# Two last products of a range's blocks done together in seven half products, in a fused attention and feed-forward kernel

## The chip, the cores and the metric

The kernel runs on one core of a Trainium2 chip. The metric is the device time of one execution in microseconds, the median of several runs; lower is better. A profile of one execution is read beside it: what each engine did and when. The engines are PE (TensorE, the matrix multiplier; its weight loads are listed as PEld), DVE (VectorE), ACT (ScalarE), POOL (GpSimd) and SP (SyncE, which here only issues DMA transfers). Each engine works through its own queue of instructions in order and waits for others by semaphores.

## What is computed

Attention over 8 batches of 12 heads, 448 positions and 64 channels, followed by a feed-forward layer with a leaky ReLU:

```python
def _attn_ref(q, k, v):
    scores = (1.0 / np.sqrt(q.shape[-1])) * np.matmul(q, k.transpose(0, 1, 3, 2))
    scores = scores - np.max(scores, axis=-1, keepdims=True)
    attn = np.exp(scores)
    attn = attn / (np.sum(attn, axis=-1, keepdims=True) + 1e-09)
    return np.matmul(attn, v).astype(np.float32)

def _moe_ref(x, w_in, w_out):
    h = x @ w_in                       # 3584 x 768 by 768 x 2048
    g = np.maximum(0.01 * h, h)
    return (g @ w_out).astype(np.float32)   # 3584 x 2048 by 2048 x 768

# x is the attention's output, (batch, position) by (head, channel)
```

Inputs and output are float32; the kernel multiplies in bfloat16 and sums in float32.

## The kernel before

**Ranges.** The 3584 tokens are cut into seven ranges (`cuts`, line 41: 0, 640, 1152, 1664, 2176, 2688, 3072, 3584). A range goes through the first layer (`head` and `neck` for range 0, `hidden(i)` for the others) and then through the second (`second(i)`). The attention of later batches is laid between the matmuls of the second layer: bursts of scores (`scores`, line 306), their exponentials on ACT (`expo`), and rows (`rows`, line 857: the weighted sums on PE, then a reciprocal and a product on DVE, then a DMA transpose from SP's queue into `xT`). `place` (line 968) decides where, with a small clock of its own, `model`, that counts what PE is given. A burst is laid only where all three slots are there and free. The kernel is written for one fixed order: each engine gets its instructions as the Python code emits them.

**PSUM.** Two single banks `g0` and `g1` (`banks`, line 66) and three tiles of two banks each, `sc0` to `sc2` (`slots`, line 67). Scores and rows use the slots, the second layer the banks, the first layer both.

**The second layer.** Blocks of 128 tokens are taken two at a time (`spots`, line 487: two pairs in each of ranges 1 to 6). For a pair, the product of 256 x 2048 by 2048 x 768 is cut in two along tokens, inner dimension and columns, and done by seven products in place of eight (the scheme of Strassen and Winograd), in `block_pair` (line 592). Each product is 8 matmuls of 128 x 128 by 128 x 384, in two accumulators `b` and `a` that alternate between the two banks. Sums of weights (`w_mix`, made once by `mix_weights` on DVE) and sums of `h` (`h_mix`, `mix_h`, and lines 621 and 627) stand in for the plain blocks. After each product DVE copies the bank to the output tile (`keep`, line 613) or adds it there (`join`, line 616), and finished tiles are stored (`store`, line 388). The seventh product multiplies the lower half of h of the pair's second block by `t4`, the third sum of weights (line 658), into the left half of the second block's output. In the last pair of all it is done in two halves of 192 columns, so that the last store is small (lines 649 to 656). Range 0 has one such pair and one done plainly (`plain_pair`).

**The first layer.** `hidden` (line 512) does the same with w_in: groups of products of 6 matmuls in two chains, one over the two banks and one over two slots, with rows laid between. Its sums of x (`x_mix`, `mix_x_part`, line 466: differences on DVE, some of 512 columns, some of 256) are emitted inside the second layer of the range before, where `model` says that the transposes of x have landed, in two parts; what is left is emitted at its end.

**The ring of x.** `xT` holds the transposed attention output, 768 channels by tokens, as a ring of `NX` = 15 x 128 tokens for each of 6 groups of 128 channels (line 103). A batch's sequence of 448 tokens that crosses the ring's end runs over into the next group's row and is copied back to the front (`OVER`, lines 108 and 469 to 473; 128 columns, emitted by `mix_x_part(3)` in the second layer of range 2).

Of the kernel before, what the change touches and what calls it, by code (L numbers as in the profile page):

```python
# [9 lines left out]
F32 = mybir.dt.float32  # L10
BF16 = mybir.dt.bfloat16
# [5 lines left out]
def kernel(  # L17
# [9 lines left out]
    nc = tc.nc  # L27

    B, H, S, D = q.shape
    DM, DF = moe_w_in.shape  # L30
    P = 128
# [4 lines left out]
    MD = DF // P  # L36
    NW = DM // 2
# [4 lines left out]
    NR = len(cuts) - 1  # L42
# [57 lines left out]
    qkb = [qkb_all[:, i] for i in range(NB)]  # L100


    NX = 15 * P

    def place_of(t):
        return (t + NX - cuts[3]) % NX

    OVER = -cuts[3] % S
    xT_flat = xT_pool.tile([P, KD * NX + OVER], BF16, name="xT")
    xT = xT_flat[:, :KD * NX].rearrange("p (k t) -> p k t", k=KD)  # L110

# [1 line left out]
    w_out_sb = w_pool.tile([P, MD, DM], BF16)  # L113
    MH = MD // 2
    w_mix = w_pool.tile([P, 3, MH, NW], BF16)
    KEEP = 4
    h = h_pool.tile([P, MD, (KEEP + 1) * P], BF16, name="h")
    h_mix = h_pool.tile([P, MH, 2, P], BF16, name="hmix")
# [305 lines left out]
    def mix_weights():  # L424
# [14 lines left out]
        for lo, hi in pieces:  # L439
            nc.vector.tensor_sub(w_out_sb[:, lo, right], w_out_sb[:, lo, right], w_out_sb[:, lo, left])  # L440
            yield

    def mix_w_in():

        near, far = slice(0, KH), slice(KH, KD)
        pieces = [(ts(c, 2 * P), slice(FH + 2 * c * P, FH + 2 * (c + 1) * P)) for c in range(FH // (2 * P))]
        for lo, hi in pieces:
            s2, s3, s4 = (w_in_mix[:, x, :, lo] for x in range(3))
            for o, x, y in (
                (s3, w_in_sb[:, near, lo], w_in_sb[:, near, hi]),  # L450
                (s2, w_in_sb[:, far, hi], s3),
                (s4, w_in_sb[:, far, lo], s2),
            ):
                nc.vector.tensor_sub(o, x, y)
                yield
        yield
        for lo, hi in pieces:
            nc.vector.tensor_add(w_in_sb[:, near, hi], w_in_sb[:, near, hi], w_in_sb[:, far, hi])
            yield
# [6 lines left out]
    def mix_x_part(i, ks):  # L466

        at = place_of(cuts[i])
        if at == 0:
            for hp in range(KD - 1) if ks.start == 0 else (KD - 1,):  # L470
                nc.vector.tensor_copy(xT[:, hp, :OVER], xT_flat[:, (hp + 1) * NX:(hp + 1) * NX + OVER])
                if hp in (1, KD - 2, KD - 1):
                    yield
        nh = (cuts[i + 1] - cuts[i]) // 2
        near, far = slice(ks.start, ks.stop), slice(KH + ks.start, KH + ks.stop)
        one, two = slice(at, at + nh), slice(at + nh, at + 2 * nh)
        t2, t3, t4 = (x_mix[:, x, near, :nh] for x in range(3))
        for o, x, y in (
            (t3, xT[:, far, two], xT[:, near, two]),
            (xT[:, near, two], xT[:, near, two], xT[:, near, one]),  # L480
            (t2, xT[:, far, two], xT[:, near, two]),
            (t4, xT[:, far, one], t2),
        ):
            nc.vector.tensor_sub(o, x, y)
            yield

    def spots(i):

        if i == 0:
            return 0, [(0, 1), (2, 3)]  # L490
        return 0, [(0, 2), (1, 3)] if cuts[i + 1] - cuts[i] == 4 * P else [(0, 1), (KEEP, 2)]

    def token(i, x):

        return KEEP * P if x == KEEP else cuts[i] + x * P

# [15 lines left out]
    def hidden(i):  # L512
# [76 lines left out]
        for m in ready:  # L589
            mix_h(i, m)  # L590

    def block_pair(i, c):

        lo, hi = slice(0, MH), slice(MH, MD)
        x1, x2 = spots(i)[1][c]
        one, two = ts(x1, P), ts(x2, P)
        s3 = h_mix[:, :, c]
        t2, t3, t4 = (w_mix[:, x] for x in range(3))
        t1 = w_out_sb[:, lo, NW:]
        left, right = slice(0, NW), slice(NW, DM)  # L600
        o1 = o_pool.tile([P, DM], F32, name="o")
        o2 = o_pool.tile([P, DM], F32, name="o")
        b, a = banks

        def product(ps, x, w, first=False, cols=slice(0, NW)):
            for m in range(MH):
                if m in (2, 4, 6):
                    yield
                nc.tensor.matmul(  # L609
                    ps[:, cols], x[:, m], w[:, m], start=(first and m == 0), stop=(m == MH - 1), skip_group_check=True,  # L610
                )

        def keep(o, at, ps, by=nc.vector.tensor_copy):
            by(o[:, at], ps[:, :NW])  # L614

        def join(o, at, ps):
            nc.vector.tensor_add(o[:, at], o[:, at], ps[:, :NW])  # L617

        yield
        yield from product(b, h[:, lo, one], w_out_sb[:, lo, left], first=True)  # L620
        nc.vector.tensor_sub(h[:, lo, one], h[:, lo, two], h[:, lo, one])
        short = cuts[i + 1] - cuts[i] < 4 * P
        keep(o1, left, b, nc.scalar.copy if c == 0 and (short or i + 1 == NR) else nc.vector.tensor_copy)
        yield
        yield from product(a, h[:, hi, one], w_out_sb[:, hi, left], first=True)
        join(o1, left, a)
        nc.vector.tensor_sub(h[:, hi, one], h[:, hi, one], h[:, lo, one])
        yield
        yield from product(b, h[:, lo, one], t2)
        keep(o1, right, b)  # L630
        yield
        yield from product(a, h[:, lo, two], t1, first=True)
        keep(o2, right, a)
        yield
        yield from product(b, s3, t3)
        join(o2, right, b)
        yield
        t0 = token(i, x2)
        last = t0 + P == B * S
        if last:  # L640
            nc.vector.tensor_copy(o2[:, NW // 2:NW], b[:, NW // 2:NW])
            store(o1, token(i, x1), left)
            store(o2, t0, right)
        yield from product(a, h[:, hi, one], w_out_sb[:, hi, right])
        join(o1, right, a)
        store(o1, token(i, x1), right if last else slice(0, DM), (nc.sync, nc.scalar if last else nc.sync))
        yield
        if last:
            w1, w2 = slice(0, NW // 2), slice(NW // 2, NW)
            yield from product(b, h[:, hi, two], t4[:, :, w1], cols=w1)  # L650
            nc.vector.tensor_copy(o2[:, w1], b[:, w1])
            store(o2, t0, w1, (nc.scalar, nc.sync))
            end = slots[0][:, 0]
            yield from product(end, h[:, hi, two], t4[:, :, w2], first=True, cols=w2)
            nc.vector.tensor_add(o2[:, w2], o2[:, w2], end[:, w2])
            store(o2, t0, w2, (nc.sync, nc.scalar))
            return
        yield from product(b, h[:, hi, two], t4)
        keep(o2, left, b)
        store(o2, t0)  # L660
        banks.reverse()
# [369 lines left out]
    def second(i):  # L1031

        x_sums = [mix_x_part(i + 1, slice(0, 2)), mix_x_part(i + 1, slice(2, 3))] if i + 1 < NR else []
        fresh, summed = [None, None], [i + 1 == NR] * 2
        left = plan[i]
        for c in range(len(spots(i)[1])):
            whole = c < plain(i)
            for x, _ in enumerate((plain_pair if whole else block_pair)(i, c)):
                fine = 1 if whole else 2
                if x % (2 * fine) == 0:  # L1040
                    advance(all(summed) or rows_done < need[i + 2])
                if c or x:
                    model["now"] += 0.65 / fine
                left -= place(i, left, calm=whole or x not in ((1, 2, 3) if i == 5 else (1, 2)), keen=need[min(i + 2, NR)], cap=NU if all(summed) else need[i + 2])
                turn_next(i)
                if whole and x in (1, 3, 5, 7):
                    mix_h(i, x - 1)
                if whole and x in (8, 9, 11, 13, 15):
                    next(outs)
                if i == 0 and c and x % 4 == 2:  # L1050
                    next(ins, None)
                for y in range(2):
                    if fresh[y] is None and i + 1 < NR and rows_done >= need[i + 2] - 1 + y:
                        fresh[y] = model["now"] + 7.0
                for y, todo in enumerate(x_sums if x % fine == 0 else ()):
                    if fresh[y] is not None and fresh[y] <= model["now"] and not summed[y]:
                        summed[y] = next(todo, 0) is not None
                        if not summed[y]:
                            break
        assert left == 0 or nxt == NU, (i, left)  # L1060
        assert i + 1 == NR or rows_done >= need[i + 2], (i, rows_done)
        for todo in x_sums:
            for _ in todo:
                pass

    ins, outs = mix_w_in(), mix_weights()
    early = [1, 2, 4, 6, 7, 9, 11]
    goals = [1, 4]
    groups, done = 0, 0
# [60 lines left out]
```

## Time and profile before

| | |
|---|---|
| time, median of 3 runs | 382.67 us (382.62 to 383.18) |
| span of the profiled execution, first to last instruction | 381.0 us |
| TensorE clock granted | 1.00 throughout |
| second layer's matmuls in pairs of blocks (L609) | 720 of 384 columns and 16 of 192; 32% of the chain |
| DVE busy | 229.9 us, of it 18 us the sums of x (L484) |
| POOL | casts of q, k, v and their loads until about 305 us of the span, then nothing |
| from the last matmul of 192 columns to the end of the span | 3.6 us: a sum on DVE (0.35), a store's issue (0.3), its landing (1.8 from its issue), the closing of the program (1.3) |

How to read the lines that follow: in the page's list of groups, a line is "line of the code, engine, operation, output<-input, shapes, count | busy us in total, mean ns of one | idle time of the engine just before them <- who ended it". In a timeline it is "start us, length us, engine, line, operation, count [idle before <- who ended it]". Matmuls are pipelined: the rows of a queue of matmuls overlap, and the pace is read from the starts. Names of buffers are shown without their numbers: `g` is a bank, `sc` a slot, `o` an output tile.

### The profile page before, as it was taken

What the parts mean: (1) busy time and instruction counts of PE and PEld (TensorE: products, weight loads), DVE (VectorE), ACT (ScalarE), POOL (GpSimd) and SP (SyncE); (2) the same over time, 40 slices, a digit from 0 to 9 for tenths busy, and PEclk for the clock granted to TensorE, in tenths of its full rate; (3) what the DMA queues carried; (4) which work ended last, traced back from release to release, by engine and by line L of the source; (5) the groups of instructions that cost most, each with busy time, mean ns of one, the idle gap of its engine ahead of it and who ended that gap; (6) DMA issues with size and microseconds to landing.
All of it is one profiled execution on the core that took longest, in us unless ns stands there. A gap on an engine that the chain in (4) does not pass through costs nothing.

```text
span 381.0 us, 9888 instructions
## 1 busy us (share of the span) xinstructions
PE 373.0 (98%) x3944; PEld 262.3 (69%) x3944; DVE 229.9 (60%) x488; ACT 254.9 (67%) x391; POOL 183.7 (48%) x376
## 2 busy tenths in 40 slices
PE   7899999999999999999999999999999999999996
PEld 3665657766598656886658866588665895668854
DVE  5663847445766646566476573765736665474753
ACT  5998885765848876478764878638787388617700
POOL 8988820996979456760576603848027100000000
PEclk9999999999999999999999999999999999999999
DMA  9999999699999759991499915999139800330022
GB/s 159 200 201 203 180 191 181 90 170 203 144 168 157 101 102 161 206 129 28 87 172 197 145 28 67 174 202 146 25 68 192 147 14 2 80 109 29 2 82 85
DMA packets 99294, 47.84 MB, mean 126 GB/s; under 512 B 63664, under 2 KB 95920, under 8 KB 99248
## 3 DMA queue, kind: packets, MB, share of 16 engines
q0 software_dynamic: 40384, 22.47, 47.9%
q1 hardware_dynamic: 58608, 24.52, 33.0%
q8 instruction: 31, 0.51, 0.5%
q10 hardware_dynamic: 256, 0.22, 0.2%
q14 instruction: 15, 0.12, 0.1%
HBM read 45.61 MB, written 11.01 MB: 149 GB/s over the span
## 4 chain that ended last, share of the span: by engine, by line
PE 93%; ACT 4%; DMA 1%; issue 1%; DVE 0%; ACTq 0%; DVEq 0%
PE g L609 32%; PE g L537 14%; PE sc L537 14%; PE sc L317 7%; PE sc L345 6%; PE g L419 4%; PE sc L314 4%; PE sc L357 3%; PE g L674 3%; ACT e L326 3%; PE g L715 2%; PE sc L338 2%; PE g L296 1%; DMA w_in_mix<-in_k_dram 1%; PE g L357 1%; ACT c L329 1%
## 5 line engine op out<-in xcount | busy, mean ns | idle before, releaser
L326 ACT ACTIVATE e<-sc 128x896 bf16<-128x896 f32 (+1 forms) x144 | 123.9, 930 | 34.0 <-PE sc L317 20.4
L609 PEld LDWEIGHTS <-h 128*128 128x128 bf16 x632 | 59.3, 98 | 44.7 <-issue 9.3
L609 PE MATMUL g<-w_out_sb,h 128*128 128x384 bf16 x416 | 78.7, 326 | 0.0
L184 POOL COPY qkb<-fq 112x512 bf16<-112x512 bf16 x36 | 24.0, 665 | 90.7 <-DMA qkT<-qkb 74.9
L526 ACT ACTIVATE h<-c 128x512 bf16<-128x512 f32 (+1 forms) x72 | 43.5, 611 | 25.2 <-DVE c L552 15.8
L537 PEld LDWEIGHTS <-w_in_sb 128*128 128x128 bf16 x576 | 54.3, 98 | 5.9
L537 PEld LDWEIGHTS <-w_in_mix 128*128 128x128 bf16 x432 | 41.2, 98 | 4.1
L873 DVE RECIPROCAL rec<-sc 112x8 f32<-112x8 f32 x42 | 8.7, 207 | 54.2 <-PE sc L345 25.9
L609 PE MATMUL g<-w_mix,h 128*128 128x384 bf16 (+1 forms) x208 | 39.0, 323 | 0.0
L614 DVE COPY o<-g 128x384 f32<-128x384 f32 x49 | 27.1, 552 | 10.4 <-PE g L609 10.1
L345 PE MATMUL sc<-v,e 128*128 128x65 bf16 x720 | 33.3, 193 | 0.0
L317 PE MATMUL sc<-qkT 64*128 64x448 bf16 (+1 forms) x210 | 32.8, 352 | 0.0
L345 PEld LDWEIGHTS <-e 128*128 128x128 bf16 x720 | 31.1, 98 | 1.4
L617 DVE TENSOR_TENSOR o<-o,g 128x384 f32<-128x384 f32 x39 | 21.6, 554 | 16.3 <-PE g L609 15.3
L874 DVE TENSOR_TENSOR x<-sc,rec 112x512 bf16<-112x512 f32 x42 | 29.0, 691 | 1.5
L537 PE MATMUL sc<-xT,w_in_sb 128*128 128x256 bf16 (+1 forms) x216 | 28.5, 268 | 0.0
L537 PE MATMUL g<-xT,w_in_sb 128*128 128x256 bf16 (+1 forms) x216 | 28.5, 268 | 0.0
L549 ACT COPY c<-g 128x512 f32<-128x512 f32 (+1 forms) x12 | 6.8, 569 | 30.8 <-PE g L537 30.8
L338 PE MATMUL sc<-v,e 128*128 128x130 bf16 x120 | 26.5, 220 | 0.0
L157 POOL DMA_DIRECT2D fv<-in_v_dram x33 | 20.6, 631 | 4.1 <-POOL v L197 2.4
L314 PE MATMUL sc<-qkT 64*128 64x448 bf16 x144 | 19.9, 357 | 2.1 <-ACT e L326 1.0
L357 PEld LDWEIGHTS <-e 112*128 112x128 bf16 x432 | 20.0, 98 | 1.8 <-issue 0.4
(131 smaller groups left out, 684.0 us busy)
## 6 DMA issues: line engine op xcount, KB each, us to landing
fq<-in_q_dram POOLq DMA_DIRECT2D x18, 224.0 KB, 5.9
w_in_sb<-in_moe_w_in_dram POOLq DMA_DIRECT2D x4, 768.0 KB, 11.2
w_out_sb<-in_moe_w_out_dram POOLq DMA_DIRECT2D x4, 768.0 KB, 19.5
out_dram<-o SPq DMA_DIRECT2D x7, 336.0 KB, 3.4
out_dram<-o SPq DMA_DIRECT2D x8, 288.0 KB, 4.0
fk<-in_k_dram POOLq DMA_DIRECT2D x15, 128.0 KB, 5.7
fv<-in_v_dram POOLq DMA_DIRECT2D x15, 128.0 KB, 4.1
out_dram<-o SPq DMA_DIRECT2D x7, 240.0 KB, 3.4
```

Of the source, the lines that this page charges most:

```text
L184: by(t[:SC, x].rearrange("p so h d -> p h so d"), f)
L314: nc.tensor.matmul(ps[:, j, :S], t[p, S + c * SC:S + c * SC + P], t[p, :S], start=True, stop=True)
L317: nc.tensor.matmul(ps[:, j, :S].rearrange("p (so s) -> p so s", so=NSC), t[p, 1, c], t[p, 0, :, :SC], start=True, stop=True,)
L326: nc.scalar.activation(e[:, :, c, :], ps[:n, :, :S], AX.Exp, scale=scale)
L338: nc.tensor.matmul(ps, e[:, EM + qc * SC:EM + qc * SC + P], vt[:, 2 * KC:].rearrange("p j d -> p (j d)"), start=True, stop=False, skip_gro ...
L345: nc.tensor.matmul(ps[:, j * (D + 1):(j + 1) * (D + 1)], e[:, at:at + P], vt[:, j * KC + c], start=False, stop=(c == KC - 1), skip_group_c ...
L357: nc.tensor.matmul(ps[:, qc, :], t[:SC, at:at + P], vt[:, c], start=(c == 0), stop=(c == NSC - 1),)
L526: nc.scalar.activation(hs[:, m:m + 2, cols], x.rearrange("p (m t) -> p m t", m=2), AX.Prelu, alpha=0.01)
L537: nc.tensor.matmul(ps[:, j * nh:(j + 1) * nh], w[:, kk, ts(j, P)], x[:, kk], start=(first and j == 0 and kk == 0), stop=(kk == KH - 1), sk ...
L609: nc.tensor.matmul(ps[:, cols], x[:, m], w[:, m], start=(first and m == 0), stop=(m == MH - 1), skip_group_check=True,)
L614: by(o[:, at], ps[:, :NW])
L874: nc.vector.tensor_mul(x, ps[:, :, :, :D], rec.to_broadcast([SC, 2, 2 * NP, D]))
```

## The change

In ranges 1 to 6 the seventh products of the two pairs share their weights, `t4`: together they are one product of 256 tokens by 1024 by 384. The change does it by seven half products once more (`deep`): each is 4 matmuls of 128 x 128 by 128 x 192, 28 in all, in place of 16 of 384 columns. The two accumulators of `deep` are the two banks of one slot, which is taken out of `slots` for that time, so that no scores are laid there. They are laid between the matmuls of the fifth and sixth product of the second pair, one half product after every two matmuls of 384 columns (in range 6 the sixth product is done in two halves of 192 columns, with its own order). After each half product DVE adds 128 x 192 numbers to an output tile.

The weights' sums for it (`mix_deep`) are made once, on POOL, in the second layer of range 1: four operations of 768 columns. The sums of h (`deep_sums`) are three DVE operations of 512 columns per range, emitted in the sixth product of the first pair, and a fourth comes in `deep`. After its fifth product a pair copies the accumulator `b` to the left half of its second output tile, where the seventh product was copied before. The first pair's second tile is kept (`kept`) until `deep` has added its part, and is stored then; its left half in range 6 goes out by POOL's queue. The order of the stores in range 6 is new.

The ring of x has 12 blocks instead of 15, and its places are counted from `cuts[5]`. The sequence that crosses the ring's end is now the third (tokens 896 to 1343, at 1152): 192 columns are copied back, in `mix_x_part(2)`, emitted in the second layer of range 1. At token 2688 the ring begins anew at the start of a sequence, without copies.

```diff
-    NX = 15 * P
+    NX = 12 * P
     def place_of(t):
-        return (t + NX - cuts[3]) % NX
+        return (t - cuts[5]) % NX
...
+    QH, QW = MH // 2, NW // 2
+    deep_mix = w_pool.tile([P, 3, QH, QW], BF16)
...
+    def mix_deep():
+        t, (t2, t3, t4) = w_mix[:, 2], (deep_mix[:, x] for x in range(3))
+        lo, hi, left, right = slice(0, QH), slice(QH, MH), slice(0, QW), slice(QW, NW)
+        sub, add = nc.gpsimd.tensor_sub, nc.gpsimd.tensor_add
+        for by, o, x, y in (
+            (sub, t3, t[:, hi, right], t[:, lo, right]),
+            (add, t2, t3, t[:, lo, left]),
+            (sub, t4, t[:, hi, left], t2),
+            (sub, t[:, lo, right], t[:, lo, right], t[:, lo, left]),
+        ):
+            by(o, x, y)
+            yield
...
+    def deep_sums(i):
+        one, two = (ts(x[1], P) for x in spots(i)[1])
+        lo, hi = slice(MH, MH + QH), slice(MH + QH, MD)
+        s3, s1 = h_mix[:, :QH, 0], h_mix[:, QH:, 0]
+        for by, o, x, y in (
+            (nc.vector.tensor_sub, s3, h[:, lo, one], h[:, lo, two]),
+            (nc.vector.tensor_add, h[:, lo, two], h[:, lo, two], h[:, hi, two]),
+            (nc.vector.tensor_sub, s1, h[:, lo, two], h[:, lo, one]),
+        ):
+            by(o, x, y)
+            yield
+
+    def deep(i):
...
+        o = [kept[i, c] for c in range(2)]
+        end = i + 1 == NR
+        slot = slots.pop(0)
+        b, a = (slot[:, x, :QW] for x in range(2))
+        for ps, first, x, w, c, cols in (
+            (b, True, h[:, lo, one], t[:, :QH, left], 0, left),
+            (a, True, h[:, hi, one], t[:, QH:, left], 0, left),
+            (b, False, s1, t2, 0, right),
+            (a, True, h[:, lo, two], t[:, :QH, right], 1, right),
+            (b, False, s3, t3, 1, right),
+            (a, False, h[:, hi, one], t[:, QH:, right], 0, right),
+            (b, False, h[:, hi, two], t4, 1, left),
+        ):
+            for m in range(QH):
+                nc.tensor.matmul(ps, x[:, m], w[:, m], start=(first and m == 0), stop=(m == QH - 1), skip_group_check=True)
+            nc.vector.tensor_add(o[c][:, cols], o[c][:, cols], ps)
+            if ps is a and first and c == 0:
+                nc.vector.tensor_sub(h[:, hi, one], h[:, hi, one], s1)
+            t0 = token(i, spots(i)[1][c][1])
+            if ps is a and not first:
+                store(o[0], t0, slice(0, NW) if end else slice(0, DM), (nc.gpsimd, nc.gpsimd) if end else (nc.sync, nc.sync))
+            if end and c == 1 and ps is b:
+                store(o[1], t0, cols, (nc.sync, nc.scalar))
+            yield
+        if not end:
+            store(o[1], token(i, spots(i)[1][1][1]))
+        slots.append(slot)
...
-        yield from product(b, s3, t3)
-        join(o2, right, b)
+        def fifth():
+            yield from product(b, s3, t3)
+            join(o2, right, b)
+            if i:
+                keep(o2, left, b)
+                if last:
+                    store(o1, token(i, x1), left)
+                    store(o2, t0, right, (nc.sync, nc.scalar))
+                elif i + 1 == NR:
+                    store(o2, t0, right)
+
+        def sixth():
+            if not last:
+                yield from product(a, h[:, hi, one], w_out_sb[:, hi, right])
+                join(o1, right, a)
+                store(o1, token(i, x1))
+                return
+            for x in range(2):
+                cols = ts(x, QW)
+                for m in range(MH):
+                    if m == QH or x and m == 0:
+                        yield
+                    nc.tensor.matmul(
+                        a[:, cols], h[:, hi, one][:, m], w_out_sb[:, hi, right][:, m, cols], start=False, stop=(m == MH - 1),
+                        skip_group_check=True,
+                    )
+                at = slice(NW + x * QW, NW + (x + 1) * QW)
+                nc.vector.tensor_add(o1[:, at], o1[:, at], a[:, cols])
+                store(o1, token(i, x1), at, (nc.sync, nc.scalar))
+
+        if i and c:
+            more = deep(i)
+            for x, _ in enumerate(fifth()):
+                yield
+                next(more)
+                yield
+            yield
+            for x, _ in enumerate(sixth()):
+                yield
+                if not last or x != 1:
+                    next(more)
+                    yield
+            yield
+            for _ in more:
+                yield
+            return
+        yield from fifth()
+        yield
+        sums = deep_sums(i) if i else ()
+        for _ in sixth():
+            next(sums, None) if i else None
+            yield
+        if i:
+            return
```

More of the change, by code (lines that the diff above doesn't have):

```diff
@@ L100 @@
     qkb = [qkb_all[:, i] for i in range(NB)]
-    NX = 15 * P
+    NX = 12 * P
     def place_of(t):
-        return (t + NX - cuts[3]) % NX
-    OVER = -cuts[3] % S
+        return (t - cuts[5]) % NX
+    OVER = max(-t % S for t in cuts if place_of(t) == 0)
     xT_flat = xT_pool.tile([P, KD * NX + OVER], BF16, name="xT")
@@ L468, in mix_x_part @@
         at = place_of(cuts[i])
-        if at == 0:
+        if at == 0 and cuts[i] % S:
             for hp in range(KD - 1) if ks.start == 0 else (KD - 1,):
@@ L590, in hidden @@
             mix_h(i, m)
+    kept = {}
+    def deep_sums(i):
[10 more added lines that the diff above has]
+    def deep(i):
+        one, two = (ts(x[1], P) for x in spots(i)[1])
+        lo, hi = slice(MH, MH + QH), slice(MH + QH, MD)
+        s3, s1 = h_mix[:, :QH, 0], h_mix[:, QH:, 0]
+        t, (t2, t3, t4) = w_mix[:, 2], (deep_mix[:, x] for x in range(3))
+        left, right = slice(0, QW), slice(QW, NW)
+        o = [kept[i, c] for c in range(2)]
[25 more added lines that the diff above has]
+        slots.append(slot)
+        model["free"][id(slot)] = model["now"] + 1.2
     def block_pair(i, c):
@@ L601, in block_pair @@
         o1 = o_pool.tile([P, DM], F32, name="o")
-        o2 = o_pool.tile([P, DM], F32, name="o")
+        o2 = kept[i, c] = o_pool.tile([P, DM], F32, name="o")
         b, a = banks
+        t0 = token(i, x2)
+        last = t0 + P == B * S
         def product(ps, x, w, first=False, cols=slice(0, NW)):
@@ L634, in block_pair @@
         yield
-        yield from product(b, s3, t3)
-        join(o2, right, b)
-        yield
[L638 to L646, printed above, removed]
@@ L647, in block_pair @@
-        yield
[L648 to L657, printed above, removed]
+        def fifth():
[8 more added lines that the diff above has]
+                    store(o2, t0, right)
@@ L1051, in second @@
                     next(ins, None)
+                if i == 1 and not c and x % 4 == 2:
+                    next(deeps, None)
                 for y in range(2):
@@ L1064, in second @@
                 pass
-    ins, outs = mix_w_in(), mix_weights()
+    ins, outs, deeps = mix_w_in(), mix_weights(), mix_deep()
     early = [1, 2, 4, 6, 7, 9, 11]
```

## The prediction

> **What bounds the kernel now.** I read the page's busy times and its shares of the chain first, then the chain in order of time, the timelines of single stretches, and the groups by shape.
>
> ```profile
> PE 373.0 (98%) x3944; PEld 262.3 (69%) x3944; DVE 229.9 (60%) x488; ACT 254.9 (67%) x391; POOL 183.7 (48%) x376
> ...
> PE 93%; ACT 4%; DMA 1%; issue 1%; DVE 0%; ACTq 0%; DVEq 0%
> ```
>
> TensorE (PE) is busy for 98% of the span and is 93% of the chain; VectorE (DVE) is 60% busy and 0% of it. So a matmul that goes saves its own time, and any wait that PE gets is lost in full. The chain in order of time (start, length, what) gives the pace of the matmuls:
>
> ```profile
> 62.90 1.82 PE g L715 x22
> ...
> 244.86 5.53 PE g L609 x34
> ...
> 376.72 0.67 PE sc L609 x8
> 377.40 0.02 issue
> 377.42 0.35 DVE o L655
> ```
>
> A matmul of 384 columns costs 5.53/34 = 0.1625 us, one of 192 columns 1.82/22 or 0.67/8 = 0.083 us. The second row is one whole end of a range (about 244.9 to 250.4), in which PE never waits. Next, how quickly work passes between PE and DVE (start, length, engine, line):
>
> ```profile
> 13.16 0.42 DVE L370 TENSOR_TENSOR x<-g,rec 112x256 bf16<-112x256 f32 x1
> 13.64 0.37 PE L384 MATMUL g<-ident,x 112*128 112x112 bf16 x4 [0.25 <-DVE x L370]
> ```
> ```profile
> 376.56 0.82 PE L609 MATMUL sc<-w_mix,h 128*128 128x192 bf16 x8
> 377.42 0.35 DVE L655 TENSOR_TENSOR o<-o,sc 128x192 f32<-128x192 f32 x1 [0.30 <-PE sc L609]
> ```
>
> PE starts 0.05 us after the DVE result that it waits for (13.58 to 13.64). DVE starts 0.04 us after the end of the last matmul's row (377.38), and that row, a pipeline's depth included, reaches 0.16 us beyond the 0.083 that PE is held. So a sum starts 0.20 us after PE has gone on. DVE in the end of a range:
>
> ```profile
> 245.23 0.56 DVE L614 COPY o<-g 128x384 f32<-128x384 f32 x1 [1.11 <-PE g L609]
> 245.70 0.41 DVE L484 TENSOR_TENSOR x_mix<-xT 128x512 bf16<-128x512 bf16 x1
> 246.15 0.61 DVE L484 TENSOR_TENSOR xT<-xT 128x512 bf16<-128x512 bf16 x1
> ...
> 251.16 0.29 DVE L484 TENSOR_TENSOR x_mix<-xT 128x256 bf16<-128x256 bf16 x1 [1.48 <-DMA xT<-x]
> ```
>
> DVE spends this end on the next range's x sums too. A row that needs nothing of the one before starts 0.08 us before that one's end (245.79 to 245.70), one that does starts 0.03 after it. The last row shows x sums waiting for a transpose, with the later rows of DVE's queue behind them. The shapes that the change uses:
>
> ```profile
> L509 DVE TENSOR_TENSOR hmix<-h 128x512 bf16<-128x512 bf16 x24 | 10.8, 452 | 1.3 <-ACT h L526 0.9
> L471 DVE COPY xT<-xT 128x128 bf16<-128x128 bf16 x6 | 1.3, 214 | 0.1
> L655 DVE TENSOR_TENSOR o<-o,sc 128x192 f32<-128x192 f32 x1 | 0.4, 354 | 0.3 <-PE sc L609 0.3
> ```
>
> **The change part by part.** I call the pairs' products P1 to P7 and the seven half products D1 to D7. In each of ranges 1 to 6 two P7 go, 16 matmuls of 0.1625 = 2.60 us. D1 to D7 come, 28 of 0.0825 = 2.31 us (0.0865, the slowest long run of the first layer's 192 wide matmuls, makes 2.42). The gain is 0.29 us a range, 1.7 in all.
>
> **The new wait.** D1 to D7 alternate between two accumulators, but both are halves of one tile, `slot`. In the program as built the first matmul of each half product waits for the DVE sum that read the half product before it (D2 for D1's, though D2 writes the other half; only D1 has no such wait). Everything behind it in PE's queue waits too. From the end of a D on PE to the earliest next D it is 0.20 + 0.355 (row L655) + 0.05 = 0.605 us; between them lie two matmuls of 384, 0.325. That alone leaves 0.28 us of idle PE five times a range (the gap D3 to D4 has four matmuls).
>
> DVE's queue makes it longer. I count from P5's start in the second pair. In ranges 2 to 4 DVE does, in this order: the copy after P4 (0.20 to 0.76), x sum (to 1.10), sum 1 (1.02 to 1.37), x sum (to 1.75), sum 2, the correction of h (0.45), x sum, sum 3, x sum, P5's join and copy (0.555 each), sum 4, sum 5, x sum, sum 6, P6's join, sum 7. So D2 starts at 1.42, not 0.98; sum 2 is 1.95 to 2.31 and D3 starts at 2.35; sum 3 ends at 3.29, in time for D4 at 3.34; sum 4 stands behind an x sum, join and copy (3.21 to 4.58) and ends at 4.96, so D5 starts at 5.01; sum 5 ends at 5.90, D6 5.95; sum 6 at 6.84, D7 6.89 to 7.22. Without waits D7 would end at 4.91. Stall 2.31, less 0.29: **+2.02 us** each, 6.1 for three. The x sum before sum 6 needs the transpose that landed 4.8 us after P5's start in the row above; one product less stands between, so 6.1 here, and D6's end rules sum 6 all the same.
>
> Range 1 has in addition the copies at the ring's seam, moved there: five of 0.25 us (192 columns, from the 0.214 of 128) before sum 3, one more later. The same count gives a stall of 2.75, **+2.46**. The old seam copies in range 2 were hidden, so taking them away gives nothing. In range 5 the x sums stand later: stall 2.04, **+1.75**. Range 6 has none, but P6 is split and its second half waits for the sum of its first, which stands behind join, copy and sum 4 (4.79, not 3.28): D7 ends at 7.32, sum 7 at 7.88. Before, the same stretch took 1.30 + 1.30 + 0.66 + 0.66 + 0.55 = 4.47, and the first pair's P7 1.30: 5.77. So **+2.10**.
>
> Between the pairs of range 6, where no attention work lies, DVE has join and copy of P5 and three sums of h (0.45 each) before P6's join. That ends 3.03 us after P5; P2 of the second pair needs that bank at 2.60. **+0.48**. In ranges 1 to 5 rows and scores (3.3 us or more) cover it; without that cover it would be 0.5 each.
>
> **The last store.** The first pair's last left half is now stored from Pool's queue, two issues. These are the only rows of such issues, the casting loads:
>
> ```profile
> L157 POOL DMA_DIRECT2D fv<-in_v_dram x33: 610/617/721, 31.7 to 289.0; - x33
> ...
> DMA to landing us min/median/max: 2.9/5.9/22.1
> ```
>
> The second issue starts at 6.94 + 0.66 = 7.6. With the least landing, 2.9, it is down at 10.5; the last SP store (sum 7 at 7.88, then 0.03, and 1.83 to landing as in the last row before) at 9.74. **+0.8**; bounds 0 (lands like SP's) and 3.8 (the median 5.9). I take the quiet end, since the queue is empty by then. The Trainium skill, "DMA: Bandwidth & Descriptors", section "Anatomy of one DMA — SWDGE (gpsimd) path", gives 2.0 us plus bytes over 436 GB/s, for 147 KB an estimate of 2.3 us. By it this term would be 0.2 and the time 0.6 lower; no run here shows a store from that queue.
>
> **At nothing.** In ranges 1 to 5 the first pair's second store moves from its P7 to D6 in SP's queue: two issues of some 0.5 us, right ahead of the second pair's own; behind them stand transposes of rows that the next range's first layer doesn't read. The output tile is held longer, but its buffer is next written in the next range's second layer, over 15 us on. ACT gets one store more at the end (0.38 us, idle there). Four weight sums go to Pool in range 1, where it idles 9.5 of 23.1 us; no row has their form. By the copies of 112x512 (0.61) they cost 4 to 8 us of Pool, ahead of that range's casts. I take 0; if casts came late it would be up to 4 once. Ring of 12: a sequence overwrites what lies 1536 tokens back, and the second layer of range i runs rows at most to the end of the sequence that holds cuts[i+2], so it hits tokens whose first layer is long done: 0.
>
> Sum: 2.46 + 6.06 + 1.75 + 2.10 + 0.48 + 0.8 = 13.65 on the execution's 381.0, 394.65. The median 382.67 lies 1.67 above that span, so **396.3**.
>
> **The rivals.**
> Bare round trip: if sums find DVE free, only 5 x 0.28 a range is lost: 6 x (1.40 - 0.29) + 0.48 = 7.1, 389.8. Against it: the order of DVE's queue is fixed, and join, copy and x sums stand in it. 0.12.
> DVE without overlap: if the rows follow each other end to start (the 0.61 row shows they can be longer beside Pool), stalls are 2.95 in ranges 2 to 4, 3.71, 2.31 and 2.58, total 17.0: 399.7. 0.15.
> Faster: the waits are met before PE reaches them, for which the round trip must fall from 0.605 to under 0.325; then 6 x 0.29 = 1.7 comes off, 380.9. The rows of 0.354 and the lags speak against it. 0.05.
> Late casts: the forecast plus 4, 400.3. 0.05.
> Clock: the first seven matmuls of 512 columns stand 0.43 us apart, half the later rate. If the idle spots brought that back, the 4.9 us of each end would double: +29, 425. Against it: three idles of 0.41 to 0.44 us between 8.6 and 10.6 us left the following pace whole. 0.03. The Trainium skill, "TensorE: Matmul & The Clock Gate", section "A second HAM failure mode: psum-queue depth-cycling", tells of such micro-idles lowering throughput; by it this rival would win, and this trace's early idles do not show it.
>
> **How the numbers follow.** The forecast's chance is 0.60, its own range 394 to 398 (the slower pitch of 192 columns adds 0.4, rows stretched beside Pool up to 1.5; the store's term may fall away, and stalls in ranges 1 to 5 may be 0.3 shorter each). The range 389.5 to 400 takes in the bare round trip and the row-by-row case and leaves out the rest. A measurement here tells 0.2% (0.8 us) from no change. Faster is its rival's 0.05, same 0.01, slower 0.94.
>
> **What would show it.** After: PE's half products with idle before each, released by DVE's 128x192 sums, five or six times a range; the stretch from P5 of the second pair to the next range about 7.2 us long, against 5.2 for P5 to P7 and the other P7; DVE without gaps there; Pool's store landing last. It is wrong if the half products follow without idle, or if PE idles elsewhere, on casts or transposes.

## The result and the profile after

The changed kernel takes 400.98 us (median of 4 runs, 399.87 to 401.95) against 382.75 before: a ratio of 1.0474, 95% interval 1.045 to 1.0497. The forecast was 396.3 with a range to 400.0: the direction is right, the loss is 4.7 us larger than forecast. The profiled execution took 401.62 with a span of 399.8, 18.8 more than before. Ratios, here and below, are of the mean times of the executions in the fast state, so they differ a little from the ratios of the medians; only the run with the last row store on SP's queue has executions outside it, two of six.

The page of the changed kernel, its busy times and its shares of the chain:

```profile
PE 377.9 (95%) x4016; PEld 266.6 (67%) x4016; DVE 252.2 (63%) x553; ACT 254.6 (64%) x391; POOL 188.8 (47%) x382
...
PE 84%; DVE 8%; ACT 4%; issue 2%; POOLq 0%; POOL 0%; DVEq 0%; ACTq 0%
```

DVE, with no share of the chain before, now has 8%: PE stands still while it waits for DVE. The view of waits says for what (engine and tile, whom it waits for: us in total, times, longest):

```profile
PE sc L644 <- DVE o L645: 6.1, 11, 1.2
PE g L678 <- DVE o L683: 2.9, 1, 2.9
```

The first row is the wait that was forecast. It is counted only where the view could follow it; the start of each matmul less the pace of the one before it gives five idle spots or so in every range. The second row, one wait of 2.9 us, was not forecast. To see where the time goes I compare when PE starts each range's first layer in the two traces (us later than before; the last two rows are the last DVE sum of the program, and the end of the span):

| start of | after, later by | of this in the range before it | forecast |
|---|---|---|---|
| range 1's first layer | -0.36 | | |
| range 2's | 6.67 | **7.03** | 2.46 |
| range 3's | 8.67 | 2.00 | 2.02 |
| range 4's | 10.67 | 2.00 | 2.02 |
| range 5's | 12.55 | 1.88 | 2.02 |
| range 6's | 14.42 | 1.87 | 1.75 |
| last DVE sum | 16.86 | 2.44 | 2.58 |
| end of the span | 18.79 | **1.93** | 0.8 |

Ranges 2 to 6 are within 0.15 of the forecast. The end of range 3 in the timeline (start, length, engine, line, operation, tiles, shapes; in brackets how long the engine was idle before and who released it):

```profile
254.70 0.35 DVE L645 TENSOR_TENSOR o<-o,sc 128x192 f32<-128x192 f32 x1
...
255.10 0.49 PE L644 MATMUL sc<-w_mix,h 128*128 128x192 bf16 x4 [0.26 <-DVE o L645]
...
257.18 0.55 DVE L686 TENSOR_TENSOR o<-o,g 128x384 f32<-128x384 f32 x1
...
257.64 0.55 DVE L683 COPY o<-g 128x384 f32<-128x384 f32 x1
258.30 0.35 DVE L645 TENSOR_TENSOR o<-o,sc 128x192 f32<-128x192 f32 x1
258.70 0.49 PE L644 MATMUL sc<-deep_mix,hmix 128*128 128x192 bf16 x4 [0.87 <-DVE o L645]
```

PE starts 0.05 us after the sum that it waits for (254.70 + 0.35, then 255.10), and the long wait is ahead of the fifth half product, whose predecessor's sum stands behind the join and the copy of the fifth product. By the pace of the matmuls PE is idle here 0.43, 0.29, 1.03, 0.28 and 0.28 us, 2.31 in all; the prediction's count gave 2.31.

Range 1 is another matter. Its second layer starts while Pool does the first three of the four new weight sums:

```profile
125.19 0.42 DVE L526 TENSOR_TENSOR h<-h 128x512 bf16<-128x512 bf16 x1
125.25 1.86 POOL L456 TENSOR_TENSOR deep_mix<-w_mix 128x768 bf16<-128x768 bf16 x1
125.79 1.61 DVE L525 TENSOR_TENSOR hmix<-h 128x512 bf16<-128x512 bf16 x1 [0.17 <-ACT h L542]
...
127.20 1.70 POOL L456 TENSOR_TENSOR deep_mix<-deep_mix,w_mix 128x768 bf16<-128x768 bf16 x1
127.43 1.75 DVE L526 TENSOR_TENSOR h<-h 128x512 bf16<-128x512 bf16 x1
128.97 1.70 POOL L456 TENSOR_TENSOR deep_mix<-w_mix,deep_mix 128x768 bf16<-128x768 bf16 x1
129.28 1.94 DVE L690 TENSOR_TENSOR h<-h 128x1024 bf16<-128x1024 bf16 x1
...
131.13 0.55 DVE L683 COPY o<-g 128x384 f32<-128x384 f32 x1
131.73 1.75 PE L678 MATMUL g<-w_mix,h 128*128 128x384 bf16 x8 [2.91 <-DVE o L683]
```

A DVE sum of 128x512 takes 0.42 where it begins before the Pool sum (first row) and 1.61 or 1.75 where it begins beside one. Each held one ends 0.3 to 0.55 us after the Pool sum does (127.11 and 127.40; 128.90 and 129.18; 130.67 and 131.22), a little less than it takes by itself (0.42, 0.42 and 0.69), and by the end of the first two the next Pool sum is under way. DVE's copy out of PSUM, L683, stands behind three of them, and PE waits for its bank. Then the granted clock falls (windows of 1 us: busy time of PE, PEld, DVE, ACT and POOL, then the clock, DMA share and GB/s):

```profile
132.00:133.00 1.00, 1.00 (x8) 0.48 (x5) 0.94 (x2) 0.00 (x0) 0.94 (x3) 0.88 0.00 0
133.00:134.00 1.00, 1.00 (x6) 0.29 (x6) 0.48 (x1) 0.00 (x0) 0.92 (x2) 0.50 0.00 0
```

PE runs at half its clock for about 3.4 us (0.24 of the first window shown, the whole of the second and of two more that are not shown, and 0.18 of the one from 136, whose clock is 0.91), and loses half of that, 1.7. With the 3.07 idle (by pace) that is 4.8, about what range 1 is over the forecast, 4.57.

### The profile page after: what moved, and what is told of

It is laid out like the page before. It is cut to its first block, busy times and chain, and to the rows that moved or that the text cites. A ratio compares the mean times of both kernels' runs of the same rounds, so it can differ in the third digit from the quotient of the medians.

```text
span 399.8 us, 10125 instructions
## 1 busy us (share of the span) xinstructions
PE 377.9 (95%) x4016; PEld 266.6 (67%) x4016; DVE 252.2 (63%) x553; ACT 254.6 (64%) x391; POOL 188.8 (47%) x382
## 4 chain that ended last, share of the span: by engine, by line
PE 84%; DVE 8%; ACT 4%; issue 2%; POOLq 0%; POOL 0%; DVEq 0%; ACTq 0%
PE g L678 22%; PE g L553 13%; PE sc L553 13%; PE sc L319 6%; PE sc L347 6%; PE g L421 4%; PE sc L316 4%; PE sc L644 3%; DVE o L645 3%; PE sc L359 3%; PE g L776 3%; ACT e L328 2%; PE g L817 2%; PE sc L340 2%; DVE o L683 1%
## 5 line engine op out<-in xcount | busy, mean ns | idle before, releaser
L678 PE MATMUL g<-w_out_sb,h 128*128 128x384 bf16 x408 | 81.5, 329 | 0.2 <-DVE o L686 0.2
L678 PEld LDWEIGHTS <-h 128*128 128x128 bf16 x520 | 48.5, 98 | 40.5 <-issue 11.0
L399 POOL DMA_DIRECT2D out_dram<-o x2 | 1.1, 542 | 76.6 <-DVE o L645 76.6
L683 DVE COPY o<-g 128x384 f32<-128x384 f32 x50 | 27.7, 553 | 12.8 <-PE g L678 12.4
L197 POOL COPY v<-fv 128x384 bf16<-128x384 bf16 x30 | 15.3, 510 | 19.3 <-PE sc L347 18.1
L678 PE MATMUL g<-w_mix,h 128*128 128x384 bf16 x112 | 21.4, 329 | 2.9 <-DVE o L683 2.9
L678 PE MATMUL g<-w_mix,hmix 128*128 128x384 bf16 x104 | 23.0, 327 | 0.0
```

The lines of the kernel that those rows point to most:

```text
L678: nc.tensor.matmul(ps[:, cols], x[:, m], w[:, m], start=(first and m == 0), stop=(m == MH - 1), skip_group_check=True,)
```

## Experiments

Each is the changed kernel with the edit shown, unless it says otherwise. The first four ran on one chip beside each other (before there: 382.9), the next four (382.61) and the last two (382.85) likewise.

**Pool's weight sums done by DVE**

```diff
-        sub, add = nc.gpsimd.tensor_sub, nc.gpsimd.tensor_add
+        sub, add = nc.vector.tensor_sub, nc.vector.tensor_add
```

> The changed kernel with one edit: the four sums of weights made by DVE instead of POOL. Theory (while POOL runs a two-input operation of 1.7 us, DVE's two-input bf16 operations do not proceed; that made the 2.9 us idle of PE at 131.7 us and the slow matmuls after it): range 1 loses about 2.5 us instead of 7.0, the time falls by 4 to 5 us, from 401 to 396 to 397, and DVE's 512 column sums there take 0.42 us, not 1.6 to 1.9. Rival (range 1 loses its 7 us to something else, the ring's copies or a store that is late): within 1 us of 401.

397.17 us (397.06 to 401.06), ratio 1.0394 (1.0356 to 1.0431). Range 1 costs 2.40 us, against 7.03 with Pool and 2.46 in the forecast; the rows below it in the table stay within 0.02. DVE's sums of 512 columns are back to 0.43 (one takes 0.71) and the one of 1024 to 0.72, the wait of 2.9 us is gone, and the clock stays at 1.00 in this stretch. The four weight sums themselves take DVE 0.85 and three times 0.54.

**Pool's weight sums in short pieces**

```diff
-            by(o, x, y)
+            for m in range(QH):
+                by(o[:, m], x[:, m], y[:, m])
```

> The changed kernel with one edit: the four sums of weights stay on POOL at the same places, but each is cut into four operations of 192 columns. If DVE is held for the length of one POOL operation, it now waits at most some 0.45 us at a time and gets in between them: PE's idle at the start of range 1's second layer falls from 2.9 us to under 1, the matmuls after it keep their pace, and the time falls by 3 to 5 us, to 396 to 398. If instead the two engines share a bandwidth, DVE is slowed over the same 7 us in all and the time stays within 1 us of 401.

397.42 us (396.85 to 399.47), ratio 1.0393 (1.0364 to 1.0422); range 1 costs 2.38. The work is still on Pool and takes it longer (9.7 us against 6.9), yet the loss is gone:

```profile
124.91 2.62 POOL L457 TENSOR_TENSOR deep_mix<-w_mix 128x192 bf16<-128x192 bf16 x4
...
125.69 0.74 DVE L526 TENSOR_TENSOR hmix<-h 128x512 bf16<-128x512 bf16 x1
126.47 0.65 DVE L527 TENSOR_TENSOR h<-h 128x512 bf16<-128x512 bf16 x1
127.28 0.80 DVE L691 TENSOR_TENSOR h<-h 128x1024 bf16<-128x1024 bf16 x1 [0.16 <-PE g L679]
127.49 2.96 POOL L457 TENSOR_TENSOR deep_mix<-deep_mix,w_mix 128x192 bf16<-128x192 bf16 x4
128.00 0.55 DVE L684 COPY o<-g 128x384 f32<-128x384 f32 x1
```

(The edit moves the lines by one.) DVE's sums now last 0.65 to 0.80: they wait for one piece (0.55 to 0.99), not for a whole sum of 1.7. So it is the length of a single Pool instruction that counts, not how much Pool reads. The rows of DVE are what shows it: range 1's cost by itself would not, since whole sums at a luckier moment gave 2.75 (below). The last row is DVE's copy out of PSUM: it takes 0.55 beside Pool as anywhere. This is what the Trainium skill says in "SBUF — State Buffer", section "SBUF: two separate sides": a DVE operation with two inputs in SBUF and a GpSimd operation that reads SBUF share a pair of ports, and the later one is shut out until the first one's instruction ends. The trace agrees, down to the copies that are spared.

**Accumulators in two tiles**

```diff
-        slot = slots.pop(0)
-        b, a = (slot[:, x, :QW] for x in range(2))
+        pair = [slots.pop(0) for _ in range(2)]
+        b, a = (x[:, 0, :QW] for x in pair)
...
```

> The changed kernel with one edit: the two accumulators of the half products lie in two slots, not in the two banks of one. Theory (each half product waits for the sum of the one before it only because both accumulators are one tile): each then waits for the sum of the half product two before, the idle before the second one (0.43 us), the third and the last two (0.29 each) goes, and what is left is the wait behind DVE's queue: 0.8 us in ranges 2 to 4, 1.5 in range 1, 0.3 in range 5, 0.9 in range 6, 5.2 in all in place of 14.1 by the same count. The time falls by about 9 us, to 392. Rival (the half products wait because DVE as such is too slow for them): the time falls by less than 3 us.

390.31 us (389.28 to 393.04), ratio 1.0201 (1.0168 to 1.0234). Ranges 2 to 6 now cost 0.46, 0.45, 0.29, 0.02 and 1.08, where they cost 2.00, 2.00, 1.88, 1.87 and 2.44. Of the idle spots of range 2 one is left:

```profile
202.21 0.55 DVE L687 TENSOR_TENSOR o<-o,g 128x384 f32<-128x384 f32 x1
...
202.67 0.55 DVE L684 COPY o<-g 128x384 f32<-128x384 f32 x1
203.33 0.81 DVE L645 TENSOR_TENSOR o<-o,sc 128x192 f32<-128x192 f32 x2
203.73 0.49 PE L644 MATMUL sc<-w_mix,h 128*128 128x192 bf16 x4 [0.58 <-DVE o L645]
```

The sixth half product adds into the accumulator that the fourth's sum must have read first, and that sum stands in DVE's queue behind the join and the copy. That is a real dependence; the four other waits came only from the shared tile. Range 1 costs 2.83 here: it has 1.9 us of idle PE behind Pool's sums, not 3.1, and the clock stays at 1.00, as the same code meets the Pool sums at another moment. So of the 10.7 us by which the time fell, some 7.9 are the tiles' in ranges 2 to 6, and the part from range 1 is not theirs alone.

**The last row store on SP's queue, not on Pool's**

```diff
-                store(o[0], t0, slice(0, NW) if end else slice(0, DM), (nc.gpsimd, nc.gpsimd) if end else (nc.sync, nc.sync))
+                store(o[0], t0, slice(0, NW) if end else slice(0, DM), (nc.sync, nc.sync))
```

> The changed kernel with one edit: the first pair's last left half in range 6 is stored from SP's queue, not POOL's. Theory (the POOL store lands later than the last SP store, and POOL's closing DRAIN of 4.5 us holds the end of the program): the time from the last sum on DVE to the end of the span falls from 5.1 to about 3.2 us, the whole by 1.9 us, to 399. Rival (the two more issues on SP push its last store back by as much): within 0.5 us of 401.

399.31 us (394.99 to 402.21, 6 runs; 398.9 over the four that the ratio counts), ratio 1.0391 (1.0352 to 1.043). The median fits the theory, but executions lie 7 us apart, so it can't carry a term of 2 us by itself; the traces do. From the last DVE sum to the end of the span it is 3.09 us here, 5.13 in the changed kernel, 3.20 before. In the changed kernel's trace the store's two issues end at 395.07, and its last piece is down at 397.06, and SP is through by 397.7. But Pool's closing instruction lasts longer (records of the trace: start, length):

```
394.472 4.507 GpSimd DRAIN
394.516 0.549 GpSimd DMA_DIRECT2D out_dram<-o
397.062 0.028 Sync EVENT_SEMAPHORE
```

It ends at 398.98 and holds the program's end. (The run took away the Pool store as a whole; that its landing alone would have cost less is read from these records, not tried.)

This profiled execution also shows one reason why the times scatter. Its range 1 costs only 2.75, with the code of that stretch unchanged:

```profile
125.48 0.42 DVE L525 TENSOR_TENSOR hmix<-h 128x512 bf16<-128x512 bf16 x1 [0.18 <-ACT h L542]
125.94 0.43 DVE L526 TENSOR_TENSOR h<-h 128x512 bf16<-128x512 bf16 x1
126.18 1.69 POOL L456 TENSOR_TENSOR deep_mix<-w_mix 128x768 bf16<-128x768 bf16 x1
...
127.07 1.34 DVE L690 TENSOR_TENSOR h<-h 128x1024 bf16<-128x1024 bf16 x1 [0.70 <-PE g L678]
127.95 1.96 POOL L456 TENSOR_TENSOR deep_mix<-deep_mix,w_mix 128x768 bf16<-128x768 bf16 x1
128.34 0.54 DVE L683 COPY o<-g 128x384 f32<-128x384 f32 x1
128.93 1.46 PE L678 MATMUL g<-w_mix,h 128*128 128x384 bf16 x8 [0.41 <-DVE o L683]
```

Pool starts 0.9 us later, DVE gets its first two sums through, one is held, and PE is idle for 0.57 by its pace. Three executions with the same code in this stretch (this one, two tiles, the changed kernel) thus give 0.57, 1.90 and 3.07 us of idle PE. What moves the moment is not shown.

**The ring of 12 blocks alone**, in the kernel before

```diff
-    NX = 15 * P
+    NX = 12 * P
```

with the two lines of the change on where a token lies in the ring.

> The kernel before with the ring of 12 blocks alone, and every last product as it was. Theory (the prediction's term of 0 for the ring): 382.7, within 0.3 of before, every range's first layer starting where it did. Rival: the ring carries a part of the loss, by other ring copies on DVE or by transposes that wait for a block that is still read; then 383.5 or more, and single ranges start later.

383.1 us (382.19 to 385.31) against 382.61 (382.11 to 384.81), ratio 1.0017 (1.0 to 1.0035). In its profiled execution range 1 starts 2.35 later than before, from one step of the scores of range 0 at 88 us (PE waits 2.06 us for a transpose into `qkT`); from there to the last sum the distance stays between 2.35 and 2.36. The ring costs nothing in ranges 1 to 6. The step at 88 us isn't something that the ring always brings: the changed kernel has this ring too, and in its profile and in those of eight of the other nine runs range 1 starts 0.2 to 0.7 us earlier than before. Why it came here is open.

**Two tiles, weight sums on DVE and the store on SP together**

The three edits above.

> Three separate edits together: accumulators in two tiles, the four weight sums on DVE, the last row store on SP's and not on Pool's queue. Theory (three separate losses that add): from the run with two tiles, whose last DVE sum stood at +4.7 against before, the 1.9 us idle in range 1's second layer goes, some 0.2 for the weight sums on DVE comes, and the end after the last sum falls from 5.65 to 3.1; span 383.9, time 385.7, half a per cent over before. Rival: the losses cover one another (with Pool's sums gone another operand is late), then 387.5 or more.

386.65 us (385.96 to 387.55), ratio 1.0097 (1.0075 to 1.0119): between the theory's 385.7 and the rival's 387.5. Range 1 costs 1.43 (2.83 with two tiles alone), the end after the last sum 0.54 over before where 2.46 was.

**The sixth product of the last range in one piece again**

```diff
-            for x in range(2):
-                cols = ts(x, QW)
...
+            yield from product(a, h[:, hi, one], w_out_sb[:, hi, right])
+            join(o1, right, a)
...
```

> The run before this one, and the last range's sixth product written again as one pass of 384 columns with one sum and one store, in place of two halves of 192 columns in one tile. Theory (a tile is one thing to wait for, whatever part of it is read): the idle 1.01 us ahead of the second half, which waits for DVE's sum of the first half, goes; 384.7, 1.0 under the run before this one. Rival: the sum of 384 columns and its store come later and hold the end, 385.7 or more.

386.23 us (385.9 to 388.0), ratio 1.0093 (1.0071 to 1.0115): 0.42 less, not 1.0, and the intervals of the two runs overlap, so the trace has to carry it. The idle spot is gone (range 6 to the last sum: 0.21, from 1.00), but 0.29 comes back after the last sum, as the rival had it.

**Two evictions on ACT**

```diff
-        keep(o2, right, a)
+        keep(o2, right, a, nc.scalar.copy if i and c else nc.vector.tensor_copy)
...
-                keep(o2, left, b)
+                keep(o2, left, b, nc.scalar.copy)
```

> The run before this one, and of the second pair of blocks two evictions (of the fourth product, and of the fifth's left part) on ACT and not on DVE. Theory (what is left of idle PE in each range, 1.2 us in range 1, 0.75 in ranges 2 and 3, 0.6 in range 4, is the half products' sums queued on DVE behind those evictions and the x sums): DVE's queue falls by 1.1 us, these gaps fall by about half, in all 1.5 to 2: 382.7 to 383.2, level with before. Rival: ACT reaches the evictions late, behind the exponentials, and PE waits for the bank; 385 or more.

385.07 us (384.55 to 387.38), ratio 1.0063 (1.004 to 1.0087): 1.16 less, where 1.5 to 2 was expected. The theory was half right. Range 1 falls to 0.63, but the idle spot ahead of the sixth half product only from 0.75 to 0.69:

```profile
199.93 0.55 DVE L687 TENSOR_TENSOR o<-o,g 128x384 f32<-128x384 f32 x1
...
200.51 0.48 ACT L684 COPY o<-g 128x384 f32<-128x384 f32 x1 [2.06 <-DVE o L687]
...
201.02 0.81 DVE L645 TENSOR_TENSOR o<-o,sc 128x192 f32<-128x192 f32 x2 [0.55 <-ACT o L684]
```

ACT's copy and DVE's join write two halves of one output tile, so the copy waits for the join, and the sum waits for the copy: the same kind of wait as the accumulators', on the output.

**The fourth half product's sum ahead of the join**

```diff
-            join(o2, right, b)
             if i:
-                keep(o2, left, b, nc.scalar.copy)
+                keep(o2, left, b)
+            if not (i and c):
+                late()
...
                 next(more)
+                if x == 0:
+                    late()
```

where `late` does the join and its stores.

> The run with evictions on ACT, with the fifth product's left part kept by DVE first, and the second pair's join of its right part after the fourth half product's sum. Theory (the sixth half product waits for the sum of the fourth, which stands behind a join of 0.55 and an eviction that ACT does after that join, as both write one tile): the idle 0.92, 0.69, 0.69 and 0.56 us ahead of the sixth half product in ranges 1 to 4 fall to 0.1 to 0.3, in all 1.8 to 2.3 less; 382.8 to 383.3. Rival: the join, now later, frees its bank or its tile late, and the idle time turns up at the next range's first product; 384.5 or more.

384.88 us (384.21 to 388.64), ratio 1.0058 (1.0036 to 1.0081), a miss: 0.2 less, not 2 (0.4 less where each is taken against the kernel before beside it), and the intervals overlap. In ranges 2 to 5 it does what was expected: they cost 0.04, 0.02, -0.02 and -0.03, so the seven half products cost no more there than the two products they replace. Range 1 (0.74, from 0.63) and range 6 with what follows it (0.11 and 1.54, from -0.03 and 0.94) took most of it back. The profiled execution lost another 1.2 us ahead of range 1, which starts 0.72 later than before where the run with evictions on ACT starts 0.46 earlier: the granted clock was 0.50 from 11.1 to 14.5 us of the span, in code that the edit doesn't touch.

**The stores of the end shared out**

```diff
-                store(o[0], t0, slice(0, NW) if end else slice(0, DM), (nc.sync, nc.sync))
+                store(o[0], t0, slice(0, NW) if end else slice(0, DM), (nc.scalar, nc.sync) if end else (nc.sync, nc.sync))
```

> The run before this one, with the store at the sixth half product's end of the last range issued by ACT and SP, one piece each, and not both by SP. Theory (of the 4.1 us between the last DVE sum and the end of the run with evictions on ACT, 0.9 over before, the part over is SP issuing seven pieces of 0.4 us one behind the other): 0.4 to 0.9 less than the run before this one, 382.2 to 382.7. Rival: the end is the landing of the last piece, whoever issues it; no difference.

384.39 us (383.93 to 385.66), ratio 1.0039 (1.0026 to 1.0051): 0.49 less, as expected (the 382.2 to 382.7 also counted on the run before coming out as forecast, which it did not); the intervals overlap, but the traces agree: the end is 1.00 over before, from 1.54. This is the fastest form found, and still 1.5 us slower than the kernel before. Its profile has 1.21 of loss in range 1 and 1.11 in range 6 and the end; none of the gain of 0.29 a range is left, as 0.33 of idle PE (0.25 and 0.08) remains in each of ranges 2 and 3.

## Why the forecast was wrong in size

**The new wait: right.** "Both are halves of one tile", "That alone leaves 0.28 us of idle PE five times a range", and the count of DVE's queue: the spots of 0.28 or 0.29 are there, and ranges 2 to 6 came out at 2.00, 2.00, 1.88, 1.87 and 2.44 against 2.02, 2.02, 2.02, 1.75 and 2.58. Two tiles took away 7.9 of these 10.2 us. The rivals of the bare round trip (1.1 a range) and of DVE without overlap (2.7) fall on these numbers.

**"At nothing", Pool's weight sums: this step failed.** "Four weight sums go to Pool in range 1 ... By the copies of 112x512 (0.61) they cost 4 to 8 us of Pool ... I take 0." Their time was sized rightly (6.9 us), and no cast was late: the view of waits has no wait of PE for one. What was left out is that another engine's instructions can't run beside them: DVE's sums with two inputs in SBUF are held until the Pool sum ends, and PE waits for what stands behind them. It cost 4.6 us in the profiled execution, 3 of them idle and the rest by the clock, and 3.8 by the medians (400.98 against 397.17 with the sums on DVE). The sign that the prediction gave of being wrong, PE idle elsewhere, came true, though not on casts or transposes. The profile before had the effect in small: of Pool's 30 copies of 128x384, 0.50 us as a rule, the one at 89.58 took 1.42, beside two DVE sums of 128x768 that began at 89.61. The prediction's +2.46 for range 1 itself was right: with Pool out of the way it is 2.40 (DVE) and 2.38 (pieces). The rival "late casts", with nearly the same time, 400.3, had another mechanism and is not what happened.

**"The last store", +0.8: the mechanism was off, and the size with it.** It cost 1.93. I reckoned with the landing, which was quicker than the least row I had: the view of DMA has 2.5 us for the piece of 144 KB and 1.8 for that of 48 KB. The Trainium skill's figure in "DMA: Bandwidth & Descriptors", section "Anatomy of one DMA — SWDGE (gpsimd) path", worked out as 2.3 for the larger piece, was near. What ends last is Pool's own closing instruction, 4.5 us from the start of the last issue on. With the store on SP it falls to -0.1.

**The ring, 0: right** for ranges 1 to 6.

**The clock: the rival's fall in every end did not come, one in range 1 did.** The rival gave the clock a fall in every range's end. In the windows over the ends of ranges 2 to 6 the granted clock stays at 1.00, with five idle spots of up to 1.03 us in each; it fell once, after 3.07 us without a matmul. The rule of the Trainium skill on micro-idles ("TensorE: Matmul & The Clock Gate", section "A second HAM failure mode: psum-queue depth-cycling"), by which the rival would win, isn't borne out in these ends. But short idles can't be called harmless: in the profile of the run "The fourth half product's sum ahead of the join" the clock fell to 0.50 at 11.1 us with no idle over 0.62 us (by pace) in the 4 us before, and with idles as long the kernel before kept 1.00 there. What decides between the two is open.

Together: 13.65 forecast, 18.79 measured; +4.57 in range 1, +1.13 after the last sum, -0.36 ahead of range 1, -0.20 in ranges 2 to 6.

What stays open: some executions of the kernels without Pool's sums are 4 us longer too (401.06 with a mean clock of 0.988 beside three of 397.1 at 0.997), and no trace of such an execution was had. The clock alone would account for it, by an estimate from these numbers: 0.009 of 399 us is 3.6 us. What brought the clock down in them isn't known.

## What to carry to other kernels

Work put on an idle engine is free only if it shares nothing with a busy one: ask which instructions of the busy engine run beside it, and if it can't be moved, cut it into short instructions, as the run with pieces of 192 columns did here. Two accumulators, or two halves of an output, that are to be used in turn belong in tiles of their own; otherwise every write waits for the read of the other half, and on a PE at 98% each such wait is lost in full. A saving of 0.29 us a range has to be weighed against the evictions it adds, here seven sums of 0.35 us and four of h a range, in a queue that PE must wait for.

## What the runs showed of the hardware

- A Pool sum of 128x768 in bf16 takes 1.6 to 2.0 us, and a DVE sum of 128x512 beside it up to 1.75 instead of 0.42; copies from PSUM beside a Pool sum stay at 0.55.
- 3.07 us without a matmul brought the granted clock to 0.50 for about 3.4 us, from some 1.0 us after the matmuls had begun again; 1.90 us did not (two tiles), nor did a wait of 2.06 us (the ring alone). One other trace had 0.50 for 3.4 us, from 11.1 us on, after idles of no more than 0.62 us.
- Pool's closing instruction lasts 4.5 us when a store was issued from its queue just before (4.51 in the changed kernel, 4.43 with two tiles), 1.9 us beyond the store's landing.
